# ScalarE's order at the head of a turn: Prelu and exp first, then the first scores' copies, then evictions

## The chip, the core and the metric

The kernel runs on one core of one Trainium2 chip. A core has four compute engines, each with an instruction queue of its own that is worked off in order: TensorE (PE in the profile, its weight loads PEld), VectorE (DVE), ScalarE (ACT) and GpSimd (POOL). SyncE (SP) issues most DMAs. TensorE writes its results to PSUM, eight banks of 512 float32 per partition, and GpSimd does not take part in reading them here: ScalarE copies them out, and a few at the end VectorE. The metric is device time of one launch in microseconds, the median of several runs; a profiled execution of the same program gives the trace.

## The reference, cut to what matters

For 8 batches and 8 heads of 576 queries and keys with 64 features, each score row keeps its 32 largest entries, a softmax is taken over them, and the values are summed. The result, 4608 tokens of 512 features, goes through a SwiGLU block.

```python
scores = scale * np.matmul(q, k.transpose(0, 1, 3, 2))
kth = np.partition(scores, -top_k, axis=-1)[..., -top_k:-top_k + 1]
scores = np.where(scores >= kth, scores, -1000000000.0)
attn = np.exp(scores - np.max(scores, axis=-1, keepdims=True))
attn = attn / (np.sum(attn, axis=-1, keepdims=True) + 1e-09)
x = np.matmul(attn, v)            # then (B,H,S,D) -> (B*S, H*D)
g = x @ w_gate
out = (g * (1.0 / (1.0 + np.exp(-g))) * (x @ w_val)) @ w_out
```

## The kernel before

**Units and turns.** The attention is cut into 160 units: 8 batches, five query tiles (qt 0 to 4, the last of 64 rows), four pairs of heads. A full unit has 128 queries of two heads; a unit of the last tile holds 64 rows of two heads side by side, so one pass of 128 rows. The 17th unit has number 16, the first one of batch 0's last tile. The main loop (L870) has a turn for each unit and three more, and each turn does different steps of several units: the selection of unit n, the softmax of unit n-1, the transposes of unit n-2, the values of units n-4 and n-3 (even turns), and the scores of units n+1 and n+2 (even turns). A batch begins at units 20, 40, and so on; so turn 20 has the first tile's scores of a new batch, while unit 19, whose softmax is due, is still one-headed.

**Steps of a unit.** scores (L288) makes four matmul products of 288 columns into four PSUM banks (L325, or L308 for the last tile) and, after its yield, four scaling copies on ScalarE (L330, L315) into the tile sc, which has three buffers. select (L333) is VectorE's: four rounds of MAX8 (L347) and three of match-and-replace (L351) into e (three buffers). shift (L357) makes the bias on POOL (L362). weigh (L367) is ScalarE's softmax: a Prelu for each head (L374), which reads sc and the 32nd largest value, and an exp for each head (L379), which reads the bias and gives the sum tot. normalize (L387) takes the reciprocal on VectorE (L392 and L393) and multiplies e on ScalarE (L397) for one head and on POOL (L399) for the other. turn (L403) transposes e on TensorE (L412), and ScalarE copies the result to et (L413). values (L423) multiplies by v (L448), and ScalarE copies the sum to xT (L465).

**Scores of an even turn.** An even turn has two sets: the *first scores* (unit n+1) are run whole at the head of the turn, the *second scores* (unit n+2) have their matmuls issued after the matmuls of the values, and their copies after weigh. All these products, the transposes and the preparation of keys and queries (prep, L257, copies at L267, L268 and L276) share one PSUM pool, ps_t, of five banks that go around in order. So the second scores use the four banks that the first scores had.

**The feed-forward block.** Its matmuls are cut into pieces (feed, L587, and piece, L777), which pieces(n) puts between the steps as far as a credit allows: a fixed order, written out when the program is built. Its products (L604, and L517 in the first blocks; L670 for the last matrix) use another PSUM pool, ps_f, of three banks. What must be done with a finished product is not issued at once: it is put on the list on_act (*evictions*: L637 to L639 and L644, or L537 to L544, for the hidden layer; L697, L704, L747, L759 for the output), and their POOL part (L540, L545, L640, L645, L657) on on_pool. flush issues all that a list holds. A turn flushes at its head, after pieces(2), after the transposes, and inside piece when more than one entry is pending.

**Order.** At the end (L942) every instruction is made to follow the one before it on its engine, so the order in which the Python code calls them is the order in each queue. Semaphores for data and buffers come on top. A turn's head is:

```python
        flush(on_act)
        flush(on_pool)
        if nxt and (n < 2 or len(nxt) > 1):
            run(nxt.pop(0))
        summed = finish_units(valued(n)) if valued(n) else no
        next(summed, None)
        if nxt:
            next(nxt[0])
        early[0]()
        if 0 <= n - 1 < NU:
            weigh(n - 1)
        run(summed)
        if nxt:
            run(nxt.pop())
```

Of the kernel before, what the change touches and what calls it, by code (L numbers as in the profile page):

```python
# [25 lines left out]
def kernel(  # L26
# [43 lines left out]
    NHP = H // 2  # L70
# [213 lines left out]
    def n_heads(qt):  # L284

        return 1 if qt == J else 2

    def scores(n):  # L288
        b, qt, hp = units[n]
        slab = preps[b * NHP + hp]  # L290
        sc = work.tile([P, 2 * S], FP32, tag="sc", name="sc", bufs=3)
        halves = [slice(0, D), slice(D, P)]
        half = S // 2

        def bank():
            return ps_t.tile([P, 512], FP32, tag="t", name="s")


        if qt == J:
            both = (slab, preps[b * NHP + hp + 1])  # L300
            banks = []
            for i in range(2):
                k0 = R + i * half
                two = [bank(), bank()]
                banks += [(i + 2 * u, ps) for u, ps in enumerate(two)]
                for u, (sl, ps) in enumerate(zip(both, two)):
                    for hh, d in enumerate(halves):
                        nc.tensor.matmul(  # L308
                            ps[halves[hh ^ u], 0:half],
                            sl[d, S + R : S + 2 * R],  # L310
                            sl[d, k0 : k0 + half],
                        )
            yield
            for i, ps in banks:
                nc.scalar.mul(sc[:, i * half : (i + 1) * half], ps[:, 0:half], scale)  # L315
            state[n + 1] = dict(sc=sc, at=S)
        else:
            q0 = S + 2 * R + qt * P
            banks = []
            for i in range(2):  # L320
                for hh, d in enumerate(halves):
                    ps = bank()
                    banks.append((i + 2 * hh, ps))
                    k0 = (1 - hh) * R + i * half
                    nc.tensor.matmul(  # L325
                        ps[:, 0:half], slab[d, q0 : q0 + P], slab[d, k0 : k0 + half]
                    )
            yield
            for i, ps in banks:
                nc.scalar.mul(sc[:, i * half : (i + 1) * half], ps[:, 0:half], scale)  # L330
        state[n] = dict(sc=sc, at=0)

    def select(n):  # L333

        nh = n_heads(units[n][1])
        sc = state[n]["sc"]
        m = small.tile([P, 2, TOP_K], FP32, tag="m", name="m")
        heads = [slice(t * S, (t + 1) * S) for t in range(nh)]
        at = state[n]["at"]
        from_ = [slice(at + t * S, at + (t + 1) * S) for t in range(nh)]  # L340
        e = work.tile([P, 2 * S], FP32, tag="e", name="e", bufs=3)
        state[n] |= dict(m=m, e=e, heads=heads, source=from_)
        cur = sc
        rounds = TOP_K // 8
        for r in range(rounds):
            for t, hs in enumerate(from_):
                nc.vector.max(m[:, t, 8 * r : 8 * r + 8], cur[:, hs])  # L347
                yield
            if r < rounds - 1:
                for t, hs in enumerate(heads):  # L350
                    nc.vector.match_replace(  # L351
                        e[:, hs], m[:, t, 8 * r : 8 * r + 8], cur[:, from_[t]], LOWEST
                    )
                    yield
                cur, from_ = e, heads
# [11 lines left out]
    def weigh(n):  # L367


        st = state[n]  # L370
        sc, m, e, heads, bias = st.pop("sc"), st.pop("m"), st["e"], st["heads"], st.pop("bias")
        tot = small.tile([P, 2], FP32, tag="tot", name="tot")
        for t, (hs, at) in enumerate(zip(heads, st.pop("source"))):
            nc.scalar.activation(  # L374
                e[:, hs], sc[:, at], AF.Prelu, bias=m[:, t, TOP_K - 1 : TOP_K], scale=-1.0,
                alpha=SMALL,
            )
        for t, hs in enumerate(heads):
            nc.scalar.activation(  # L379
                e[:, hs], e[:, hs], AF.Exp, bias=bias[:, t : t + 1], scale=-1.0 / SMALL,  # L380
                accum_out=tot[:, t : t + 1],
            )
        if n < AHEAD:
            nc.scalar.add(tot[:, 0 : len(heads)], tot[:, 0 : len(heads)], EPS)
        st["tot"] = tot

    def normalize(n):  # L387
        st = state[n]
        tot, e, heads = st.pop("tot"), st["e"], st.pop("heads")
        nh = len(heads)  # L390
        for t in range(nh if n >= AHEAD else 0):
            nc.vector.tensor_scalar_add(tot[:, t : t + 1], tot[:, t : t + 1], EPS)  # L392
        nc.vector.reciprocal(tot[:, 0:nh], tot[:, 0:nh])  # L393
        yield
        for t, hs in enumerate(heads):
            if t == 0 and n >= 3 * NHP:
                nc.scalar.mul(e[:, hs], e[:, hs], tot[:, t : t + 1])  # L397
            else:
                nc.gpsimd.tensor_tensor(  # L399
                    e[:, hs], e[:, hs], tot[:, t : t + 1].to_broadcast([P, S]), ALU.mult  # L400
                )
# [83 lines left out]
    on_act, on_pool = [], []  # L485

    def flush(queue):
        while queue:
            queue.pop(0)()
# [280 lines left out]
    NU = len(units)  # L770
# [33 lines left out]
    def fetch(n):  # L804

        b, qt, hp = units[n]
        i = b * NHP + hp
        if qt == 0:
            yield from prep(i)
        if qt == J and i + NHP < len(pairs):  # L810
            load(i + NHP)

    def share(n):


        others = 0.0
        for m, cost in [(m, 0.7) for m in valued(n)] + [(n - TURN, 0.6)]:
            if m >= 0:
                others += cost * (0.5 if units[m][1] == J else 1)
        others += 0.7 * len(scored(n))  # L820
        if units[n + 3][1] == 0:
            others += 0.6

        beside = 5.8 if n < AHEAD else 6.25
        least = 2.0 if n >= 3 * NHP and n % 2 == 0 else 0.0
        return max(least, beside * n_heads(units[n][1]) / 2 - others)

    def scored(n):

        ahead = [n + 1] if n < 2 else [] if n % 2 else [n + 1, n + 2]  # L830
        return [m for m in ahead if m < NU and (units[m][1] < J or m % 2 == 0)]

    def valued(n):

        behind = [] if n % 2 else [n - 4, n - 3]
        return [m for m in behind if 0 <= m < NU]
# [6 lines left out]
    def run(steps):  # L843
        for _ in steps:
            pass
# [24 lines left out]
    for n in range(NU + 3):  # L870
        nh = n_heads(units[n][1]) if n < NU else 1
        topk = select(n) if n < NU else no
        norm = normalize(n - 1) if 0 <= n - 1 < NU else no
        nxt = [scores(m) for m in scored(n)]
        ahead = fetch(n + 3 if n else 2) if n + 3 < NU else no

        def dve(k, beside=True):

            for _ in range(k * nh):
                next(topk, None)  # L880
                due[0] += 5 / 6 if beside else 0
                if due[0] >= 1 and not (n == 0 and len(steps) == 5):
                    due[0] -= 1
                    steps.append(n)
                    rounding(1)

        if n >= NU - NHP:
            credit[0] = 8.0
        else:
            credit[0] = min(credit[0] + share(n), share(n) + 1)  # L890
        flush(on_act)
        flush(on_pool)
        if nxt and (n < 2 or len(nxt) > 1):
            run(nxt.pop(0))
        summed = finish_units(valued(n)) if valued(n) else no
        next(summed, None)
        if nxt:
            next(nxt[0])
        early[0]()
        if 0 <= n - 1 < NU:  # L900
            weigh(n - 1)
        run(summed)
        if nxt:
            run(nxt.pop())


        dve(2, beside=False)
        if n == 0:
            run(ahead)
            load(3)  # L910
            ahead = fetch(3)
        if n < NHP:
            load_v(n)
        pieces(2)
        flush(on_act)
        dve(1)
        dve(1)
        if 0 <= n - TURN < NU:
            run(turn(n - TURN))

        flush(on_pool)
        next(ahead, None)
        pieces(1)
        next(ahead, None)
        dve(1)
        pieces(1)
        if n < AHEAD:
            run(topk)
        run(norm)
        run(topk)  # L930
        if n < NU:
            shift(n)
        pieces(6)
# [50 lines left out]
```

## Time and profile before

| | |
|---|---|
| Median of 3 runs | 1712.43 us (1711.92 to 1713.5) |
| Profiled execution: time, span | 1712.03 us, 1710.2 us |
| Mean granted TensorE clock | 0.978 |
| PE busy | 1647.4 us, 96% |
| DVE busy | 1476.5 us, 86% |
| ACT busy | 1259.5 us, 74% |
| POOL busy | 799.0 us, 47% |

The span is from the first to the last instruction; the time has some 2 us more around it. Busy times count an engine's instructions, not its waits. A line of the waits reads: engine, its tile and line, the one it waited for, total us, number of waits, the longest. In a timeline a line is the start in us, the length of the merged group, engine, line, operation, tiles, shapes, and the count; in brackets the idle time before it and what ended it. A matmul of float32 leaves two records, a transpose one.

### The profile page before, as it was taken

The numbers are of one execution on the slowest core, as the hardware profiler recorded it, in microseconds if no ns is written. First come the engines' busy times: TensorE is split into PE (matmuls) and PEld (weight loads), VectorE is DVE, ScalarE is ACT, GpSimd is POOL, SyncE is SP. The second block draws the span as 40 slices with busy tenths as digits, with TensorE's granted clock in tenths as the row PEclk, the third lists the DMA queues.
The fourth block names the chain that finished last, engine by engine and source line by source line (L and its number), as shares of the span: only waits on it lengthen the run. The fifth ranks groups of instructions, "written<-read, shape, count | busy, mean of one in ns | idle before, by whom it ended". The sixth has DMA issues, their size and how long they took to land.

```text
span 1710.2 us, 32128 instructions
## 1 busy us (share of the span) xinstructions
PE 1647.4 (96%) x11600; PEld 1398.2 (82%) x11600; DVE 1476.5 (86%) x3311; ACT 1259.5 (74%) x2901; POOL 799.0 (47%) x914
## 2 busy tenths in 40 slices
PE   5588999999999999999999999999999999999999
PEld 3477698987888887888888888888888888888887
DVE  7999899998989899997999989998999979999400
ACT  7899887877767787768676887777777778676531
POOL 4798545352444425353535334444344433535434
PEclk6699999999999999999999999999999999999999
DMA  7533120003000030001200030000400011000000
GB/s 210 139 112 99 29 72 2 14 1 79 22 13 1 15 86 14 1 8 42 51 14 1 13 74 27 2 13 2 98 1 13 2 44 29 13 2 13 1 13 13
DMA packets 109310, 59.74 MB, mean 35 GB/s; under 512 B 88544, under 2 KB 96992, under 8 KB 109152
## 3 DMA queue, kind: packets, MB, share of 16 engines
q1 hardware_dynamic: 108016, 57.37, 12.9%
q8 instruction: 91, 1.49, 0.4%
q14 instruction: 67, 0.55, 0.1%
q10 hardware_dynamic: 1136, 0.33, 0.1%
HBM read 48.23 MB, written 9.44 MB: 34 GB/s over the span
## 4 chain that ended last, share of the span: by engine, by line
PE 88%; DVE 5%; ACT 4%; DMA 1%; POOL 1%; issue 1%; SPq 0%; POOLq 0%; ACTq 0%
PE f L604 37%; PE x_ps L670 10%; PE av L448 9%; PE s L325 8%; PE y_ps L670 8%; PE etps L412 7%; PE f L517 6%; DVE m L347 2%; DVE e L351 2%; PE kqps L271 1%; PE o_ps L569 1%; PE s L308 1%; ACT e L379 1%; DVE size L124 1%; ACT e L374 0%
## 5 line engine op out<-in xcount | busy, mean ns | idle before, releaser
L347 DVE MAX8 m<-e 128x8 f32<-128x576 f32 x864 | 617.9, 755 | 3.3
L351 DVE MATCH_REPLACE8 e<-m,e 128x576 f32<-128x576 f32 x576 | 425.4, 748 | 0.0
L604 PE MATMUL f<-xT,wg 128*128 128x256 f32 x1440 | 335.9, 382 | 1.3 <-ACT xT L465 1.3
L604 PE MATMUL f<-xT,wv 128*128 128x256 f32 x1440 | 331.4, 380 | 0.0
L604 PEld LDWEIGHTS f<-xT,wg 128*128 128x128 f32 x1440 | 268.9, 190 | 49.0 <-issue 13.1
L604 PEld LDWEIGHTS f<-xT,wv 128*128 128x128 f32 x1440 | 268.2, 190 | 37.5 <-issue 3.8
L640 POOL TENSOR_TENSOR h<-h,half_g 128x512 f32<-128x512 f32 x90 | 114.7, 1275 | 349.2 <-ACT h L639 349.2
L330 ACT ACTIVATE sc<-s 128x288 f32<-128x288 f32 x512 | 170.4, 431 | 105.2 <-PE s L325 104.6
L413 ACT COPY et<-etps 128x512 f32<-128x512 f32 (+1 forms) x448 | 183.6, 486 | 66.0 <-PE etps L412 65.6
L379 ACT ACTIVATE e<-e,bias 128x576 f32<-128x576 f32 x288 | 221.7, 780 | 12.7 <-POOL bias L362 9.7
L374 ACT ACTIVATE e<-sc,m 128x576 f32<-128x576 f32 x288 | 212.3, 792 | 0.6 <-DVE m L347 0.5
L351 DVE MATCH_REPLACE8 e<-m,sc 128x576 f32<-128x576 f32 x288 | 212.6, 748 | 0.0
L412 PE MATMUL etps<-ident,e 128*128 128x128 f32 x1312 | 178.2, 280 | 33.7 <-POOL e L399 15.0
L347 DVE MAX8 m<-sc 128x8 f32<-128x576 f32 x288 | 204.0, 747 | 7.5 <-ACT sc L330 7.5
L412 PEld LDWEIGHTS etps<-ident,e 128*128 128x128 f32 x1312 | 156.2, 144 | 54.7 <-POOL e L399 19.2
L645 POOL TENSOR_TENSOR h<-h,val 128x512 f32<-128x512 f32 x90 | 114.8, 1275 | 155.0 <-ACT val L644 152.4
L325 PE MATMUL s<-kqT 64*128 64x288 f32 x1024 | 169.2, 441 | 13.7 <-ACT sc L330 7.5
L399 POOL TENSOR_TENSOR e<-e,tot 128x576 f32<-128x576 f32 x140 | 161.1, 1154 | 28.5 <-DVE tot L393 28.2
L448 PE MATMUL av<-et,v 128*64 128x128 f32 (+1 forms) x2560 | 158.0, 268 | 0.0
L448 PEld LDWEIGHTS av<-et,v 128*64 128x64 f32 x2560 | 137.7, 140 | 5.9 <-ACT kqT L268 2.7
L325 PEld LDWEIGHTS s<-kqT 64*128 64x128 f32 x1024 | 94.2, 190 | 58.3 <-issue 18.4
L397 ACT ACTIVATE e<-e,tot 128x576 f32<-128x576 f32 x148 | 119.1, 805 | 21.7 <-DVE tot L393 21.6
(86 smaller groups left out, 2249.1 us busy)
## 6 DMA issues: line engine op xcount, KB each, us to landing
v<-in_v_dram SPq DMA_DIRECT2D x32, 256.0 KB, 3.3
kq_in<-in_k_dram SPq DMA_DIRECT2D x63, 128.0 KB, 2.8
kq_in<-in_q_dram SPq DMA_DIRECT2D x63, 128.0 KB, 2.9
w<-in_moe_w_gate_dram SPq DMA_DIRECT2D x12, 512.0 KB, 3.8
w<-in_moe_w_val_dram SPq DMA_DIRECT2D x12, 512.0 KB, 3.8
w<-in_moe_w_out_dram SPq DMA_DIRECT2D x12, 512.0 KB, 3.5
out_dram<-o SPq DMA_DIRECT2D x38, 128.0 KB, 2.4
out_dram<-o SPq DMA_DIRECT2D x16, 256.0 KB, 2.5
```

Source lines behind the costliest of these rows:

```text
L325: nc.tensor.matmul(ps[:, 0:half], slab[d, q0 : q0 + P], slab[d, k0 : k0 + half])
L330: nc.scalar.mul(sc[:, i * half : (i + 1) * half], ps[:, 0:half], scale)
L347: nc.vector.max(m[:, t, 8 * r : 8 * r + 8], cur[:, hs])
L351: nc.vector.match_replace(e[:, hs], m[:, t, 8 * r : 8 * r + 8], cur[:, from_[t]], LOWEST)
L374: nc.scalar.activation(e[:, hs], sc[:, at], AF.Prelu, bias=m[:, t, TOP_K - 1 : TOP_K], scale=-1.0, alpha=SMALL,)
L379: nc.scalar.activation(e[:, hs], e[:, hs], AF.Exp, bias=bias[:, t : t + 1], scale=-1.0 / SMALL, accum_out=tot[:, t : t + 1],)
L399: nc.gpsimd.tensor_tensor(e[:, hs], e[:, hs], tot[:, t : t + 1].to_broadcast([P, S]), ALU.mult)
L412: nc.tensor.transpose(ps[:, c * P : (c + 1) * P], e[:, k0 : k0 + P], ident[:])
L413: nc.scalar.copy(et[:, c0 : c0 + cn, :], ps[:, 0 : cn * P].rearrange("p (c j) -> p c j", c=cn),)
L448: nc.tensor.matmul(av[d, i, 0:ql], weights_, moving, start=c == (0 if last else J), stop=c == (J if last else J - 1),)
L604: nc.tensor.matmul(ps[:, i, :], w[:, kc, m * P : (m + 1) * P], x[:, kc, :], start=(kc == 0), stop=(kc == KC - 1),)
L670: nc.tensor.matmul(ps, lhsT, T[i][m], start=m == 0, stop=m == MQ - 1)
```

## The change

From turn 16 on (n >= 4 * NHP, with NHP = 4), as long as there is a unit n-1, weigh(n - 1) is called first in the turn, then the first scores if the turn has two sets, and only then are the pending evictions flushed, and POOL's list after them. The later call of weigh is left out in these turns. In turns before 16 weigh stays where it was, and flush(on_act) is called ahead of the first scores, as before; the last two turns have no weigh.

```diff
             credit[0] = min(credit[0] + share(n), share(n) + 1)
+        ahead_of = n >= 4 * NHP and n - 1 < NU
+        if ahead_of:
+            weigh(n - 1)
+        else:
+            flush(on_act)
+        if nxt and (n < 2 or len(nxt) > 1):
+            run(nxt.pop(0))
         flush(on_act)
         flush(on_pool)
-        if nxt and (n < 2 or len(nxt) > 1):
-            run(nxt.pop(0))
         summed = finish_units(valued(n)) if valued(n) else no
         next(summed, None)
         if nxt:
             next(nxt[0])
         early[0]()
-        if 0 <= n - 1 < NU:
+        if 0 <= n - 1 < NU and not ahead_of:
             weigh(n - 1)
         run(summed)
```

## The prediction

> **What bounds the kernel now.** I read the page's busy shares and chain first, then busy time by stretches of the run, then the waits, then the timeline of single turns.
>
> ```profile
> PE 1647.4 (96%) x11600; PEld 1398.2 (82%) x11600; DVE 1476.5 (86%) x3311; ACT 1259.5 (74%) x2901; POOL 799.0 (47%) x914
> PE 88%; DVE 5%; ACT 4%; DMA 1%; POOL 1%; issue 1%; SPq 0%; POOLq 0%; ACTq 0%
> ```
>
> TensorE is the bound and carries the chain. Its idle time is 1710.2 - 1647.4 = 62.8 us, but by stretches of the run 38.3 us of that lie before 100 us, 12.3 between 100 and 200, 1.4 between 200 and 300. The change starts at turn 16, at 194 us, so it can touch little idle time:
>
> ```profile
> 900.00:1100.00 200.00, 200.00 (x1370) 168.94 (x1368) 180.89 (x414) 148.67 (x345) 86.60 (x105) 1.00 0.10 25
> ```
>
> (The columns after the length are PE, PEld, DVE, ACT and POOL busy.) TensorE has no gap at all in these 200 us. Next the waits, PE's own after 195 us, then two of the whole run (total us, times, longest):
>
> ```profile
> PE etps L412 <- ACT e L397: 3.5, 2, 1.8
> PE s L325 <- ACT et L413: 2.0, 3, 1.0
> PE f L604 <- ACT xT L465: 1.3, 1, 1.3
> ```
>
> ```profile
> ACT sc L330 <- PE s L325: 104.6, 39, 5.6
> DVE tot L392 <- ACT e L379: 101.1, 85, 9.3
> ```
>
> With three smaller lines TensorE waits for others 8.4 us in all from turn 16 on. The large waits, ScalarE's 104.6 us in front of the score copies and VectorE's 101.1 us for the exp's sum, are on engines that are not the bound. They are what the new order can remove. What TensorE can gain is at most those 8.4 us, plus some tenths of slow pacing beside them.
>
> [...]
>
> **The change, part by part.** Instructions of an engine run in program order, so the records can be counted off turn by turn. ScalarE's part at the head of an even turn n was: pending evictions, four copies of the first scores (unit n+1), Prelu and exp of unit n-1, xT copy, four copies of the second scores (n+2). It becomes: Prelu and exp, first scores, evictions, xT copy, second scores. Nothing is added or removed; the order on PE, DVE, POOL and SP, DMA issues included, is the same.
>
> *Prelu and exp moved to the front.* They need the unit's last maximum (DVE), and exp also the bias (POOL). Turn 90, from 914.5 us:
>
> ```profile
> 915.56 0.20 POOL L362 TENSOR_TENSOR bias<-m 128x2 f32<-128x2 f32 x1 [1.31 <-DVE m L347]
> 917.98 1.24 PE L325 MATMUL s<-kqT 64*128 64x288 f32 x8
> 918.77 1.32 ACT L330 ACTIVATE sc<-s 128x288 f32<-128x288 f32 x4 [4.24 <-PE s L325]
> 919.94 1.46 ACT L374 ACTIVATE e<-sc,m 128x576 f32<-128x576 f32 x2
> 921.49 1.24 PE L325 MATMUL s<-kqT 64*128 64x288 f32 x8
> ```
>
> The bias stands at 915.76, ScalarE idles until TensorE's scores at 918.77, and Prelu and exp take 2.85 us (919.94 to the xT copy at 922.79). In front they run in the idle time, from 915.5 to about 918.4, and the copies begin at 918.8 as before. TensorE's second scores need the first copy's bank; that is freed at 919.2 and wanted at 921.49. Free for TensorE, 4.5 us earlier for VectorE's sum. Most of VectorE's 101 us goes so. What is late next for it is its e buffer (38.5 us of waits for L412's transposes already), which is TensorE's own pace: no gain in the time.
>
> *First scores behind Prelu and exp.* The five banks of ps_t go around: four first scores, one for the values, and the second scores reuse the first four. The copies of the first scores are what the second scores wait for. I made the sum of turn 90 for each of the 56 turns with first scores from turn 20 on: ScalarE free, or last maximum and bias ready; plus 2.85 us; then the copies; against the start of the second scores. In 47 turns 0.2 to 2.5 us are left over. Nine come out short. Seven are alike, turns 20, 40, ... 140, where a new batch begins; turn 100:
>
> ```profile
> 1009.94 0.83 ACT L397 ACTIVATE e<-e,tot 128x576 f32<-128x576 f32 x1
> 1010.62 1.36 ACT L330 ACTIVATE sc<-s 128x288 f32<-128x288 f32 x4
> 1011.78 0.86 ACT L374 ACTIVATE e<-sc,m 128x576 f32<-128x576 f32 x1
> 1011.87 1.24 PE L325 MATMUL s<-kqT 64*128 64x288 f32 x8
> 1012.73 0.78 ACT L379 ACTIVATE e<-e,bias 128x576 f32<-128x576 f32 x1
> 1013.04 1.56 PE L670 MATMUL y_ps<-wo,h 128*128 128x256 f32 x6
> 1013.50 0.24 ACT L465 COPY xT<-av 128x128 f32<-128x128 f32 x1
> ```
>
> Here ScalarE has run without a gap since 1007.6 (copies of et, of the new slab, the L397 product), and goes straight into the copies. The one-headed Prelu and exp take 1.72 us (1011.78 to 1013.50). In front, they hold the copies until 1012.34. The first bank is free at 1012.34 + 0.43 = 1012.77, 0.90 later than TensorE wants it (1011.87); the fourth copy ends at 1013.70, the fourth pair of matmuls a third of a us later, near 1014.0, against 1013.04 before: 0.97. I take 0.95 a turn, 7 x 0.95 = 6.7 us, bounds 0.6 (first bank alone, releases at their fastest) and 1.1. TensorE has nothing else to do in between, so all of it is on the path.
>
> The eighth is turn 66, the one place where VectorE is behind TensorE:
>
> ```profile
> 673.20 1.29 ACT L330 ACTIVATE sc<-s 128x288 f32<-128x288 f32 x4
> 673.78 1.42 DVE L347 MAX8 m<-e 128x8 f32<-128x576 f32 x2
> 674.10 1.24 PE L325 MATMUL s<-kqT 64*128 64x288 f32 x8
> 677.73 2.86 PE L604 MATMUL f<-xT,wg 128*128 128x256 f32 x12 [1.32 <-ACT xT L465]
> ```
>
> The last maximum ends at 675.20. VectorE lost 1.7 us two units earlier to the sum's wait, of which I expect 0.8 back (then its e buffer binds, at 665.6). So Prelu and exp end near 676.7, the first bank is free at 677.1 and TensorE, wanting it at 674.1, waits 3.0; the 1.3 us at 677.73 go in return. Net +1.7. Bounds: -2.7 (VectorE recovers wholly, and this wait and the 1.16 us at 670.92 vanish) and +3.9 (it recovers nothing). The ninth, turn 68, is 0.4 short; VectorE's recovery should cover half: +0.2.
>
> *Evictions last.* 54 turns have any at the head, one to four instructions. They come up to 8 us later. Behind them wait the ps_f bank (three go around; the smallest margin to its next matmul is 1.9 us, at turn 121, most are 4 to 10) and POOL's products (TensorE reads those 11 us later or more; the bias and the L399 products that follow in POOL's queue lose 2 to 3 us at turns 82 and 134, before their turn's transposes). One pending eviction, L759 at turn 160, has stores in SP's queue behind its POOL sum; its copy comes within 0.2 us of the old time, and so do they. Priced at nothing; if the cover were gone, a late eviction would cost the rest of a weigh, at most 2.9 us each.
>
> [...]
>
> *The end.* At 1643.02 TensorE waits 1.78 us for L397, which hangs on the last exp. Prelu starts 1.76 us earlier there, but L397 then stands behind the et copies, which end near 1641.9: -0.4. The 1.75 us wait at 395.77 stays, since turn 36 has neither evictions nor first scores at its head.
>
> Sum: 6.7 + 1.7 + 0.2 - 0.4 = +8.2. On the profiled execution's 1712.03 that is 1720.2; the runs' median is 0.4 above it: 1720.6.
>
> **The rivals.**
> *Faster.* One mechanism: VectorE's 101 us turn into a lead, so that turn 66's lag goes (-2.7), and copies at batch starts find ScalarE earlier, since L397 no longer waits for the sum (21.6 us in all). It decides if ScalarE at 1010.6 is 0.95 us earlier in all seven turns. Against it: ScalarE is gapless from 1007.6, and before that waits for TensorE's transposes. With the 0.4 at the end and 2 of the other waits: -5, 1707.
> *No change.* The batch starts cost 0.6 each (+4.2) and turn 66 gives 2.7 back: +1.1 with the end, 1713.5. For it: both are bounds of rows above; against: both must hold at once.
> *Much slower.* Prelu waits for VectorE in more turns, each holding the copies some 3 us as in turn 66. From eight such turns on, +24 on the 8, 1744. Against it: VectorE is ahead by 1 to 7 us in nearly all turns and gains.
>
> **How the numbers follow.** My forecast 0.63, faster 0.11, no change 0.17, much slower 0.09. 0.2% is 3.4 us, about what a measurement of this kernel can tell from no change. The forecast's own range is 1716 (7 x 0.6, turn 66 even) to 1724 (7 x 1.1, turn 66 at +3.9). For 8 in 10 I go from 1709.5, which takes in no change and part of the gains, to 1728, with two of the extra turns. Faster 0.11, same 0.17, slower 0.72.
>
> **What would show it.** Right: waits of PE s L325 for ACT sc L330 at seven batch starts, about 0.9 us each; ACT sc L330's 104.6 us and DVE tot L392's 101.1 us down to a fraction; DVE e L351's wait for L412 up. PE's busy time itself unchanged. Wrong: no such wait at 1012; waits of PE f L604 or of POOL's readers for evictions; ACT e L374 waiting for DVE m in many turns.

## The result and the profile after

The changed kernel takes 1724.08 us (median of 6 runs, 1723.68 to 1725.47) against 1713.08 us for the kernel before beside it: a ratio of 1.0063, interval 1.0052 to 1.0073, some 11 us slower. The profiled execution took 1723.68 us with a span of 1721.9, 11.7 us more than before's 1710.2.

The page's busy shares and the chain's first line:

```profile
PE 1652.6 (96%) x11600; PEld 1403.4 (82%) x11600; DVE 1472.5 (86%) x3311; ACT 1264.9 (73%) x2901; POOL 799.7 (46%) x914
PE 86%; DVE 6%; ACT 5%; issue 1%; POOL 1%; DMA 1%; SPq 1%; ACTq 0%; POOLq 0%; DVEq 0%
```

TensorE still has nearly all of the chain, with two points of it now VectorE's and ScalarE's. Its busy time is 5.2 us longer with the same 11600 matmul records, and its idle time (span less busy time) 6.5 us: 69.3 in place of 62.8.

The waits after 195 us, of TensorE, VectorE and ScalarE (total us, times, longest):

```profile
PE s L325 <- ACT sc L330: 8.9, 8, 3.0
...
DVE e L351 <- PE etps L412: 111.5, 61, 5.9
...
DVE tot L392 <- ACT e L379: 45.4, 22, 6.8
...
ACT sc L330 <- PE s L325: 32.5, 46, 2.3
...
ACT e L379 <- POOL bias L362: 29.1, 15, 4.0
```

The first line is new; before had no such wait from 195 us on. The other four are the change at work off the bound. Before had there:

```profile
DVE e L351 <- PE etps L412: 38.5, 18, 3.9
...
ACT sc L330 <- PE s L325: 103.4, 37, 5.6
```

VectorE's wait for the sum is down from 101.1 to 45.4 us, its wait for the e buffer up from 38.5 to 111.5; ScalarE's wait in front of the score copies is down from 103.4 to 32.5, its wait for the bias up from 6.9 to 29.1. None of that shortens the run.

TensorE's instructions are the same in the same order, so its time can be compared turn by turn (from a turn's first matmul to the next turn's). Up to turn 16 the two executions differ by 0.04 us. From there, after less before:

| Turns | after less before, us |
|---|---|
| 20 | +1.53 |
| 40, 60, 80, 100, 120, 140 | +1.29 each, +7.75 |
| 66 | +4.81 |
| 24, 35 | +0.26, +0.22 |
| 27; 71, 89 and 107; 160 | -0.57; -0.27 each; -0.37 |
| all other turns to 160 | +0.36 |
| from turn 161 to the end | -1.49 |
| sum | +11.7 |

Turn 100, timeline, where the old order is shown in the prediction:

```profile
1020.42 0.82 ACT L374 ACTIVATE e<-sc,m 128x576 f32<-128x576 f32 x1
...
1022.11 1.29 ACT L330 ACTIVATE sc<-s 128x288 f32<-128x288 f32 x4
...
1022.55 1.65 PE L325 MATMUL s<-kqT 64*128 64x288 f32 x8 [0.81 <-ACT sc L330]
...
1024.13 1.56 PE L670 MATMUL y_ps<-wo,h 128*128 128x256 f32 x6
```

Prelu starts where the copies used to start. The copies come 1.69 us behind it, and TensorE's second scores, which the view has waiting 0.81 us, start 3.80 us after the turn's first matmul (1018.75) where they started after 2.91 (1008.96 to 1011.87): 0.89 us later. They then take 1.58 us (1022.55 to 1024.13) where they took 1.17 (1011.87 to 1013.04): 0.41 us more. The two add up to the turn's 1.29. The 0.41 is seen in the single records. The timeline at the first start, 1011.86 to 1011.88 in before and 1022.50 to 1022.56 here:

```profile
1011.87 0.51 PE L325 MATMUL s<-kqT 64*128 64x288 f32 x2
...
1022.55 0.51 PE L325 MATMUL s<-kqT 64*128 64x288 f32 x1 [0.81 <-ACT sc L330]
```

In before the eight records of the four products start two at a time, in four steps. Here the products start 0.30 us apart, behind copies that start 0.29 us apart and free the banks; the first record and the last (1022.55 and 1023.80) have no partner, and the four steps become five.

Turn 66, timeline, and the busy time of the stretch behind it (PE, PEld, DVE, ACT, POOL, then the granted clock):

```profile
677.26 1.41 DVE L347 MAX8 m<-e 128x8 f32<-128x576 f32 x2
...
680.90 1.28 ACT L330 ACTIVATE sc<-s 128x288 f32<-128x288 f32 x4
681.35 2.58 PE L325 MATMUL s<-kqT 64*128 64x288 f32 x8 [3.00 <-ACT sc L330]
...
683.86 5.71 PE L604 MATMUL f<-xT,wg 128*128 128x256 f32 x16
```

```profile
680.00:690.00 10.00, 8.65 (x30) 6.86 (x31) 9.91 (x22) 4.33 (x15) 0.00 (x0) 0.66 0.00 1
682.00:687.00 5.00, 5.00 (x15) 3.62 (x13) 4.97 (x15) 1.93 (x7) 0.00 (x0) 0.50 0.00 2
```

VectorE's last maximum ends at 678.67, Prelu and exp hold the copies until 680.90, and TensorE waits 3.00 us. Behind that its clock is halved (0.50 from 682 to 687): 0.66 over 10 us is 6.8 us at half speed (2 x 0.34 x 10). Sixteen L604 matmuls take 5.71 us here, 3.62 elsewhere (before, at 905.85 and 1610.40).

### The profile page after: what moved, and what is told of

Read it like the earlier page. It is cut to its first block, busy times and chain, and to the rows that moved or that the text cites. A ratio compares the mean times of both kernels' runs of the same rounds, so it can differ in the third digit from the quotient of the medians.

```text
span 1721.9 us, 32156 instructions
## 1 busy us (share of the span) xinstructions
PE 1652.6 (96%) x11600; PEld 1403.4 (82%) x11600; DVE 1472.5 (86%) x3311; ACT 1264.9 (73%) x2901; POOL 799.7 (46%) x914
## 3 DMA queue, kind: packets, MB, share of 16 engines
q8 instruction: 91, 1.49, 0.4%
## 4 chain that ended last, share of the span: by engine, by line
PE 86%; DVE 6%; ACT 5%; issue 1%; POOL 1%; DMA 1%; SPq 1%; ACTq 0%; POOLq 0%; DVEq 0%
PE f L604 36%; PE x_ps L670 10%; PE av L448 8%; PE s L325 8%; PE y_ps L670 7%; PE etps L412 7%; PE f L517 5%; DVE m L347 2%; DVE e L351 2%; ACT e L379 1%; PE o_ps L569 1%; PE kqps L271 1%; PE s L308 1%; DVE size L124 1%; ACT et L413 1%
## 5 line engine op out<-in xcount | busy, mean ns | idle before, releaser
L604 PE MATMUL f<-xT,wg 128*128 128x256 f32 x1440 | 337.1, 383 | 0.0
L604 PE MATMUL f<-xT,wv 128*128 128x256 f32 x1440 | 331.4, 380 | 0.0
L604 PEld LDWEIGHTS f<-xT,wg 128*128 128x128 f32 x1440 | 270.0, 191 | 48.1 <-issue 13.4
L604 PEld LDWEIGHTS f<-xT,wv 128*128 128x128 f32 x1440 | 268.3, 190 | 37.5 <-issue 3.8
L374 ACT ACTIVATE e<-sc,m 128x576 f32<-128x576 f32 x288 | 211.3, 786 | 8.2 <-DVE m L347 7.9
L325 PE MATMUL s<-kqT 64*128 64x288 f32 x1024 | 175.5, 448 | 21.9 <-ACT sc L330 15.4
L330 ACT ACTIVATE sc<-s 128x288 f32<-128x288 f32 x512 | 169.4, 421 | 34.6 <-PE s L325 33.8
L325 PEld LDWEIGHTS s<-kqT 64*128 64x128 f32 x1024 | 99.7, 192 | 67.0 <-issue 21.6
L397 ACT ACTIVATE e<-e,tot 128x576 f32<-128x576 f32 x148 | 119.6, 808 | 12.9 <-DVE tot L393 12.8
```

The costliest lines, as they stand in the source:

```text
L325: nc.tensor.matmul(ps[:, 0:half], slab[d, q0 : q0 + P], slab[d, k0 : k0 + half])
L374: nc.scalar.activation(e[:, hs], sc[:, at], AF.Prelu, bias=m[:, t, TOP_K - 1 : TOP_K], scale=-1.0, alpha=SMALL,)
L604: nc.tensor.matmul(ps[:, i, :], w[:, kc, m * P : (m + 1) * P], x[:, kc, :], start=(kc == 0), stop=(kc == KC - 1),)
```

## The experiments

Theory, the *held bank*: the loss is TensorE's second scores waiting for the first scores' copies, which now stand behind Prelu and exp, at the seven batch starts and in turn 66, with the clock's drop on top there. Rival, *late evictions*: what costs is that evictions come last, through ps_f banks or POOL's queue. In the diffs a minus is the changed kernel.

**Copies first.**

```diff
         ahead_of = n >= 4 * NHP and n - 1 < NU
-        if ahead_of:
-            weigh(n - 1)
-        else:
+        if not ahead_of:
             flush(on_act)
         if nxt and (n < 2 or len(nxt) > 1):
             run(nxt.pop(0))
+        if ahead_of:
+            weigh(n - 1)
         flush(on_act)
```

> The head of a turn becomes first scores' copies, Prelu and exp, evictions. Theory of the held bank (the loss is TensorE's second scores waiting for the first scores' copies behind Prelu and exp): both terms go, the seven batch starts (7 x 1.1 us) and turn 66 (some 5 us); 1711 to 1714 us, level with before, with no wait of PE s L325 for ACT sc L330 after 195 us. Rival, late evictions: they still stand behind Prelu and exp, so most of the 11 us stays, 1721 to 1724.

Measured: 1711.76 us against 1713.3, ratio 0.9995 (0.9986 to 1.0004). TensorE's waits after 195 us no longer name the score copies of L330; the three largest that are left are ones that before had:

```profile
PE etps L412 <- ACT e L397: 3.1, 2, 1.7
PE s L325 <- ACT et L413: 2.0, 3, 1.0
PE f L604 <- ACT xT L465: 1.3, 1, 1.3
```

Evictions stand behind Prelu and exp as in the changed kernel, and cost nothing that the time shows; the largest losses by turns are 0.5 us, in turns 27 and 63. One pair of neighbours in ScalarE's order, Prelu and exp ahead of the first scores' copies, makes the whole difference.

**Evictions first.** Only the evictions go back to the front.

```diff
         ahead_of = n >= 4 * NHP and n - 1 < NU
+        flush(on_act)
         if ahead_of:
             weigh(n - 1)
-        else:
-            flush(on_act)
         if nxt and (n < 2 or len(nxt) > 1):
             run(nxt.pop(0))
-        flush(on_act)
         flush(on_pool)
```

> The head becomes evictions, Prelu and exp, first scores' copies. Held bank: the copies come later still; by the old trace eleven more turns (22, 32, 42, 48, 50, 62, 70, 88, 106, 122, 124, those with a gate's three evictions) fall short by 1.4 to 2.5 us, 19 us together, on top of the 11: about 1742 us. Late evictions: the evictions are back in front, so the loss goes: 1713.

Measured: 1756.33 us, ratio 1.0254 (1.024 to 1.0268).

```profile
PE s L325 <- ACT sc L330: 27.0, 19, 3.0
```

The rival said 1713. The wait for the copies grows from 8 times to 19, the eleven turns that were named among them, and those cost 29.5 us together where 19 were expected. Seven of them cost 1.8 to 2.0 us each; turns 22, 42, 62 and 106 cost 3.5 to 4.4, and each of these four has one drop of the granted clock (0.83 over the 10 us from 250, 451, 660 and 1117, 3.4 us each at half speed). Turn 37 is 1.4 us longer with another such drop (0.83 from 404 to 414). So the evictions' place matters in the other direction: behind Prelu and exp they leave ScalarE free early, ahead of them they hold the copies further.

**Batch starts as before.**

```diff
-        ahead_of = n >= 4 * NHP and n - 1 < NU
+        ahead_of = n >= 4 * NHP and n - 1 < NU and n % (5 * NHP)
```

> The changed kernel, but turns 20, 40, ... 140 (batch starts) have the old order. Held bank: 7 x 1.1 us come back, 1724.1 - 8.0 = 1716, and the one wait of PE s L325 for ACT sc L330 that is left is turn 66's 3.0 us. Late evictions: these turns have no evictions at their head, so nothing changes, 1724.

Measured: 1715.19 us, ratio 1.0014 (1.0005 to 1.0024): 8.9 us less than the changed kernel. The edit gives turn 160 its old order too, which is worth 0.4 us the other way. One wait for the copies is left, turn 66's; the turn costs 3.5 us in this execution, where the clock's drop is 3.4 us long (0.83 from 676 to 686):

```profile
PE s L325 <- ACT sc L330: 3.0, 1, 3.0
```

**Turn 66 as before.**

```diff
-        ahead_of = n >= 4 * NHP and n - 1 < NU
+        ahead_of = n >= 4 * NHP and n - 1 < NU and n != 66
```

> The changed kernel, but turn 66 alone has the old order. Held bank with the clock: the 3.0 us wait at 681 goes, the granted clock stays at 1.0 around it, and a wait of TensorE for the xT copy of 1 us or so comes back: 1724.1 - 5 = 1719, at most 1720. If the clock's drop there has another cause than the wait, the drop stays and only some 2 us are won: 1722. Late evictions: turn 66 has none, no change, 1724.

Measured: 1720.17 us, ratio 1.0041 (1.0026 to 1.0057), 3.9 us less than the changed kernel. In the profiled execution the turn is 0.7 us shorter than in before, and the granted clock is 1.00 from 676 to 690. But that execution has a drop elsewhere, behind the 1.75 us wait for L397 of turn 37, which before and the changed kernel have too, there at full clock (1.00 from 396 to 406 in both):

```profile
396.00:406.00 10.00, 8.26 (x73) 6.98 (x72) 9.46 (x20) 9.42 (x24) 0.85 (x3) 0.83 0.34 77
```

Turn 37 is 1.43 us longer with that.

**Both as before.** The two edits together (`n % (5 * NHP) and n != 66`).

> The changed kernel, but the seven batch starts and turn 66 have the old order; the other turns keep Prelu and exp first, evictions last. Held bank: the two terms are all of the loss, so it is gone: 1724.1 - 8.9 - 3.9 = 1711.3, level with before or up to 2 us better. Late evictions: 46 turns or so still have their evictions behind Prelu and exp, so part of the loss should be left, some 1717 or more.

Measured: 1711.89 us, ratio 0.9994 (0.9985 to 1.0003). The two terms are all of the loss: with eight turns (and turn 160) put back, the other turns, taken together, are no slower than before, evictions last and all. They are not measurably faster either. (By turns, turn 66 is 0.7 us shorter than in before, and turn 68 0.7 longer.)

**Evictions second.** Prelu and exp stay as in before; pending evictions go behind the first scores' copies.

```diff
-        ahead_of = n >= 4 * NHP and n - 1 < NU
-        if ahead_of:
-            weigh(n - 1)
-        else:
+        ahead_of = False
+        if n < 4 * NHP:
             flush(on_act)
```

> Prelu and exp stay where they were before; only the pending evictions move behind the first scores' copies (head: copies, evictions, Prelu and exp). Held bank: nothing, 1712 to 1714. Late evictions: slower than before, by up to a few us.

Measured: 1716.11 us, ratio 1.0018 (1.0009 to 1.0027): some 3 us slower, which the theory had not expected.

```profile
PE x_ps L670 <- POOL xT L677: 3.5, 3, 1.2
```

Three waits, in turns 71, 89 and 107, 1.2 us each (+1.16 in the comparison by turns); turns 27 and 63 lose 0.5 each. It isn't an eviction that comes too late. In turn 88 ScalarE used to clear the eviction of a gate while it waited for TensorE's scores; now the copies go first, and the eviction runs between them and Prelu, which starts 3.9 us after the turn's first matmul where it started at 2.8. The sum comes 1.2 us later, with it VectorE's unit, the bias in POOL's queue (20.1 against 18.9 us) and the L677 differences behind the bias, for which TensorE waits. Copies first, where the evictions stand later still but behind the exp, has none of these waits. So in this kernel a late *exp* has a price in three turns; the changed order, whose exp is early, gains 0.27 us in the same three.

**Batch starts alone.** Before's order, with Prelu and exp first where `n % (5 * NHP) == 0`, which takes in turn 160.

> Before's order everywhere, but Prelu and exp first in turns 20, 40, ... 140 alone. Held bank: the seven waits alone, 7 x 1.1 us + 0.2 = +8, 1721, with seven or eight waits of PE s L325 for ACT sc L330 of 0.8 to 1.0 us. Late evictions: no change, 1713.

Measured: 1721.46 us, ratio 1.0048 (1.0034 to 1.0062), +8.2 us.

```profile
PE s L325 <- ACT sc L330: 5.9, 7, 1.0
```

By turns: +1.52 at turn 20, +1.28 or +1.29 at the six others, and no other turn of 16 to 159 differs by over 0.2 us. The same prices as inside the changed kernel: what the other turns do has no part in them.

**Odd turns alone.** Before's order, with Prelu and exp ahead of the evictions where `n % 2 == 1`.

> Prelu and exp first in odd turns alone, where there are no first scores and only evictions stand behind them. Held bank: no loss, 1711 to 1714. Late evictions: most of the turns with evictions at the odd heads still pay, some 3 to 5 us slower than before, 1717.

Measured: 1713.34 us, ratio 0.9999 (0.999 to 1.0008). Of the turns from 16 to 160 none differs by more than turn 35, 0.20 us.

**Turn 66 alone.** Before's order, with the new one where `n == 66`.

> Before's order everywhere, with Prelu and exp first in turn 66 alone. Held bank with the clock: VectorE has won nothing in the turns ahead, so its last maximum comes some 0.7 us later against TensorE than in the changed kernel; PE s L325 waits 3.5 to 3.9 us once for ACT sc L330, the 1.3 us wait for xT goes, and the clock halves for one window or two behind it (1.7 to 3.4 us): +4 to +6 us, 1717 to 1719. Without a share of the clock it is +2.5 us, 1716.

Measured: 1717.18 us, ratio 1.0023 (1.0014 to 1.0032), +3.8 us; by turns +3.98 in turn 66 and less than 0.2 in every other turn of 16 to 160.

```profile
PE s L325 <- ACT sc L330: 3.7, 1, 3.7
```

```profile
672.00:680.00 8.00, 3.66 (x46) 3.04 (x47) 7.97 (x19) 5.73 (x14) 2.62 (x3) 0.98 0.17 66
680.00:690.00 10.00, 10.00 (x47) 8.33 (x47) 9.97 (x24) 5.91 (x16) 2.00 (x2) 0.85 0.01 2
```

The wait is 3.70 us, 0.7 more than in the changed kernel: the 0.7 is what VectorE had won there. At half speed, the 0.50 of the changed kernel's drop, were 0.3 us of the first stretch and 3.0 of the second (2 x 0.02 x 8 and 2 x 0.15 x 10), one drop of some 3.4 us. The 1.7 to 3.4 us that were expected for the clock are half of the two lengths measured until then, 3.4 us in batch starts as before and 6.8 in the changed kernel. With a longer wait the turn still costs less than the 4.81 us of the changed kernel's execution, where the drop was twice as long.

**Prelu first, exp behind the copies.** weigh gets a yield between its Prelus and its exps, and its later call, for the turns before 16, runs it to the end. The turn's head:

```diff
         if ahead_of:
-            weigh(n - 1)
+            softmax = weigh(n - 1)
+            next(softmax)
         else:
             flush(on_act)
         if nxt and (n < 2 or len(nxt) > 1):
             run(nxt.pop(0))
+        if ahead_of:
+            run(softmax)
         flush(on_act)
```

> From turn 16 the head is Prelu, first scores' copies, exp, evictions: the hold in front of the copies is cut from 1.72 to 0.95 us at batch starts (one Prelu) and from 2.85 to 1.4 us elsewhere. Held bank: the cost of a batch start falls by the 0.77 us, from 1.29 to some 0.5 us, 3.6 us for seven; turn 66 waits some 2 us for the copies, gets 1.3 back, and the clock may or may not drop: with the gains at turns 27, 71, 89, 107 and 160 some 1715, at most 1719. Late evictions: they come no earlier than in the changed kernel, so 1724.

Measured: 1715.17 us, ratio 1.0011 (1.0001 to 1.0021). With the shorter hold a batch start costs 0.33 or 0.34 us where it cost 1.29. Turn 100, timeline:

```profile
1014.09 1.58 PE L325 MATMUL s<-kqT 64*128 64x288 f32 x8
1015.60 1.13 PE L671 MATMUL y_ps<-wo,h 128*128 128x256 f32 x4
```

The second scores start 2.91 us after the turn's first matmul (1011.18), as in before, since the first copy ends in time (1013.97); but they take 1.51 us where they took 1.17, as the second product has to wait for the second copy (its start is 1014.32, the copy's end 1014.27) and the records no longer start in pairs. The view shows no wait here, as the first product keeps TensorE busy; the whole loss is the slower pace. Turn 66 waits 1.5 us:

```profile
PE s L325 <- ACT sc L330: 1.5, 1, 1.5
```

With this wait the clock stays at 1.00 from 672 to 692, and the turn is 0.5 us longer than before's.

## Why the prediction was right, point by point

**Direction and mechanism held.** Forecast 1720.6, measured 1724.08, at the upper end of the 1716 to 1724 that the forecast gave itself, with +8.2 on the profiled execution against +11.7. The loss is at the places that were named: PE s L325 waiting for ACT sc L330 at the seven batch starts and in turn 66, eight waits in all. Taking the two places back brings 1711.89, and each alone has its price. That the total came so near is in part luck: the two terms came out at 14.1 us where 8.4 stood, and 1.5 us of the excess went again with a clock drop at the end that before's execution had and this one had not, which no term foresaw.

**Batch starts: 6.7 forecast, 9.3 measured.** The mis-sized step is the end of the second scores. I had the fourth copy end and a third of a us of matmul behind it, 0.97 in sum, and took 0.95. Measured is a start 0.89 us late, as the working had it (0.90), and second scores slowed by 0.41, for which the working left 0.07: TensorE goes on 0.73 us after the last copy's end (1023.40 to 1024.13), not 0.33. A third of a us is one step; the last product's two records run one after the other and take two, 0.68. Turn 20 is dearer (1.53) by a start 1.12 us late: the sum's L384 (0.20 us) stands in front of its copies too.

**Turn 66: +1.7 forecast, +4.8 measured,** beyond the bound of +3.9. The wait itself was 3.00 us, as forecast, and VectorE recovered 0.7 us of its lag (6.0 us behind TensorE's turn in before, 5.3 here) where I had 0.8. The wait for xT did go. What failed is that the wait was priced at its own length: the clock was halved for 6.8 us behind it (0.66 from 680 to 690, 0.50 from 682 to 687), which costs at most 3.4 us, and the slower pace of the second scores comes on top as at the batch starts. The runs bear out the clock's part. With the turn back in its old order the drop is gone (1.00 from 676 to 690), alone in before's order it has a drop again (0.85 from 680 to 690), and with a 1.5 us wait it has none (1.00 from 672 to 692). The +4.8 is one execution's; the same 3.0 us wait cost 3.5 with a drop half as long, and by the medians turn 66 is worth 3.9 (put back) or 3.8 (alone).

**Turn 68 and the small margins.** The 0.4 that turn 68 was short did not show: it is among the turns that differ by less than 0.2 us. In the kernel with turn 66 put back it does show, as a wait of 0.2 us and +0.7. Of the 47 turns with something left over, none has a wait for the copies. The tightest is turn 24, where the first copy ends 0.21 us ahead of the second scores' start: they start on time and take 0.25 us longer, the turn's +0.26. Turns 142, 44 and 52, with 0.37 to 0.39, lose less than 0.2.

**Evictions at nothing** held: copies first and odd turns alone, both with evictions behind Prelu and exp, are level with before.

**The end: -0.4 forecast,** -0.37 measured at turn 160 and -1.49 behind it. The 1.78 us wait is down to 1.41. The rest is the clock: before had a drop there, the changed kernel none (0.83 from 1640 to 1650 against 1.00 from 1650 to 1664). Half of the 3.4 us is 1.7. Batch starts as before and evictions second, which have the old 1.78 us wait and no drop, are 1.48 and 1.50 shorter there too. Whether the earlier exp spares the drop or the moment does, the runs leave open: of the profiled executions, none of the five with the new order in turn 160 and a shorter wait had one at the end, and five of the seven others had.

**The rivals.** *Faster* needed ScalarE 0.95 us earlier at batch starts. It came at 1020.42 against 1010.62, which is 9.8 us later, while TensorE's first scores came 9.79 later (1018.75 against 1008.96): no earlier at all, and VectorE's 101 us, of which 56 went, bought 1 to 2 us. *Much slower* needed Prelu to hold the copies for VectorE's sake in eight more turns; ACT e L374 waits for DVE m eight times, 7.9 us in all, but a TensorE wait came of it only in turn 66. *No change* fell with both of its bounds.

## What to carry to other kernels

When work moves ahead of an evacuation in an in-order queue, don't ask how long the queue idles on average, but turn by turn when the freed bank is next wanted: 47 of 56 turns had room for 2.85 us, and seven that looked alike, with the shorter 1.72 us in front, had not. Nor is it enough that the first bank is free in time: where the later ones come at the copies' pace, the products lost 0.25 to 0.34 us a turn here, without a wait in the view. Time won on engines that only follow the bound went into other waits of theirs here: VectorE's for the sum fell by 56 us, its wait for the e buffer rose by 73. And a wait of the bound engine can cost more than its length: the 3.00 us of turn 66 cost 4.81, with the clock at 0.50 behind it. Count what its clock does there.

## What the runs showed of the hardware

**The clock behind a wait.** From turn 16 to the last 10 us, the changed kernel's execution has one drop in the granted clock, 0.66 over the 10 us from 680, and before's has one, 0.83 over the 10 us from 1640. Inside both it is 0.50 (682 to 687, 1644 to 1647); counted at that half speed, the first is 6.8 us long and the second 3.4, as is every drop of 0.83 over 10 us below. In the one of turn 37, turn 66 as before, eight L271 products took 1.91 us where they took 1.04 in the changed kernel.

Waits of TensorE of 3.0 us had a drop of 6.8 us behind them (changed kernel) or of 3.4 (batch starts as before: 0.83 from 676 to 686), 3.7 us had one of 3.4 (turn 66 alone), 1.5 us had none in one execution (Prelu first: 1.00 from 672 to 692). The same 1.75 us wait of turn 37 had none in before or the changed kernel (1.00 from 396 to 406) and one in two other programs (0.83 from 396 to 406 in turn 66 as before, from 404 to 414 in evictions first). In evictions first alone, waits of 1.32 us had a drop in turn 106 (0.83 from 1117 to 1127) and none in turns 48, 50, 70, 88 and 124. So in these runs the length of a wait alone did not decide. What else did was not shown: no run here varies the moment of a wait alone.

**Matmuls paced by evacuation.** In turn 100, four products of 64 rows took 1.17 us where their records started two at a time (before), 1.58 us where each waited for its own bank (changed kernel), and 1.51 us where only the first bank was free in time (Prelu first). In the second case the engine went on 0.73 us after the last copy.
